# Cosine attention and a low-rank mixer on one core: token tiles regrouped to 3, 1 and twelve pairs, and unit vectors of three batches moved from VectorE to GpSimd

## The chip, the core and the metric

The kernel runs on one core of one Trainium2 chip. The metric is the device time of one execution in microseconds; the median of several runs counts. A profiled execution gives the trace that all tables here come from. "PE" is TensorE's matmul side and "PEld" its weight loads, "DVE" is VectorE, "ACT" ScalarE, "POOL" GpSimd and "SP" the engine that issues most DMAs.

## The reference

Inputs are q, k and v of shape 8 x 12 x 448 x 64 (batch, head, sequence, head dimension), U (448 x 32), V (32 x 448), w1 (768 x 3072) and w2 (3072 x 768), all in fp32.

```
q_n = q / (norm(q) + 1e-6);  k_n = k / (norm(k) + 1e-6)
attn = softmax(q_n @ k_n^T / tau)             # tau = 0.1
x = (attn @ v), heads side by side            # 8 x 448 x 768
u = x + (x^T @ U @ V)^T                       # mixing along the sequence, rank 32
out = u + relu(u @ w1) @ w2
```

## The kernel before

Attention runs batch by batch. For each batch q and k are loaded by GpSimd's DMA queue as tiles of 112 rows (4 sequence positions a row), the squares are made on ScalarE or VectorE, VectorE reduces them, and a square root by logarithm and exponential and a reciprocal give the inverse norms. `norm` (line 690) then multiplies each pair of heads by its inverse norms: two VectorE products of 112 x 512 for each pair (line 702), six pairs a batch. Batches 0 and 1 turn the unit vectors with TensorE transposes (`flip`, line 544); later batches with a DMA transpose issued by SP (line 717). Scores are matmuls with 64 rows (line 763), ScalarE takes the exponential (line 781), values are matmuls with 65 columns whose last column is the sum (line 808), and VectorE divides by it (reciprocal, line 837, and product, line 839).

`stage0` (line 904) makes u from x: a projection with U (line 916), its result A copied to SBUF, matmuls with V (line 967), and an addition to x (line 976). u is stored to DRAM by SP (line 1005) and comes back in two ways: as rows (line 870) and as columns through a DMA transpose (line 866). For batch 1 the columns are made on TensorE instead (`flip` again, its matmuls on line 556), straight into the one buffer `uT`.

Two batches are 896 positions, 7 tiles of 128; the 28 tiles of all batches go through the MLP in units. A *plain* unit (`mlp`, line 1337) has 24 x 6 up matmuls (line 1352) over all its tokens and, for each tile, 2 x 24 down matmuls of 384 columns (line 1394). A *half* unit has two tiles: its up part is plain (144 matmuls of 256 columns, line 1240), and its down part is Strassen-Winograd: 7 products of 12 matmuls of 384 columns (line 1269) in place of 8, with sums of relu blocks (lines 1212 to 1214 and 1223) and of w2 blocks (line 1061). ScalarE copies the first product (line 1292), GpSimd adds u to it three times (line 1294), VectorE adds the other products (line 1287). A *full* unit combines w1 in the same way too (252 up matmuls of 128 columns, line 1133). Before the change the tiles go as two plain units of 3, six half units and five full ones (`PLAIN`, `HALF`). The `relu` buffer and the `uT` buffer are single; `mlp` for one tile puts four blocks of 128 columns into one PSUM bank.

The combined w2 blocks T1, T2, T4 take room that attention no longer needs. The class `Shrink` is a ring of buffers that gives up some of them after a number of uses (`WHOLE` batches); `Gone` is what waits for those uses. T1 lies where two buffers of u rows were, T2 in the third buffer of loaded q and k, in one of unit vectors and in the end of `uT`, T4 in one of squares, two of transposed unit vectors, one of A and a part of `relu`.

The order of all instructions is found ahead of time by a planner (`Plan.run`): each operation has an engine, an assumed duration, dependencies, buffers to acquire and release, and a priority. On PE there are ten streams in order of preference, attention first and the MLP last, so the MLP fills what attention leaves. On GpSimd the additions of line 1294 go ahead of the loads. What the planner gives is one fixed order for each engine, and each engine works through its own in order, waiting where it must. This holds for the issue of DMAs too.

Of the kernel before, what the change touches and what calls it, by code (L numbers as in the profile page):

```python
# [309 lines left out]
def kernel(  # L310
# [27 lines left out]
    PE_BATCHES = 2  # L338
    LATE, VLATE = 6.0, 2.8
    BURST = [1] + [2] + [3] * 6  # L340
    PLAIN = [3, 3]
    HALF = 6
    WHOLE = 4
    LAST = {0: 0, 2: 2, 4: 4}, {0: 0, 2: 0, 4: 4}
    WIDE = 1
    TB = 2
# [18 lines left out]
    def fixed_ring(tiles):  # L365
# [24 lines left out]
    X_t = const.tile([128, 2 * 4 * C], BF, name="X_sb")  # L390
    r_X = fixed_ring([X_t[:, 4 * C * i:4 * C * (i + 1)].rearrange("p (t c) -> p t c", t=4) for i in range(2)])
    A_t = const.tile([128, 3, C], BF, name="A_sb")
    r_A = Shrink([A_t[:, i, :] for i in range(3)], WHOLE, (0, 1))
    r_gone, r_gone2 = Gone(r_ld, r_xn), Gone(r_sq, r_qkT, r_A)
    u_t = const.tile([128, 8, C], BF, name="u_nat")
    r_ur = Shrink([u_t[:, i, :] for i in range(3)], 3, (0, 1))
    dram = ctx.enter_context(tc.tile_pool(name="dram", bufs=1, space=bass.MemoryType.DRAM))
# [4 lines left out]
    w2_t = const.tile([128, NC, C], BF, name="w2_sb")  # L402
    relu_t = const.tile([128, NC * 512], BF, name="relu")
    views = [relu_t.bitcast(FP)[:, 0:4 * R + S + 4 * SC * D]] + [
        relu_t[:, 0:NC * n].rearrange("p (f n) -> p f n", f=NC) for n in (512, 384)] + [None]
    r_relu = Ring(1, lambda i: views[min(i, 3)])
    uv = Slot(r_relu, 6)

# [91 lines left out]
    pe_sc = plan.stream("PE")  # L500
    pe_mlp = plan.stream("PE")
    pool_y = plan.stream("POOL")
    pool_q = plan.stream("POOL")
    plan.keep = pe_sc, r_sc, (0, 1, 2, 3, 4, 5)

# [6 lines left out]
    def dve_t(n, fast=1, fixed=0.065):  # L512
        return fixed + n * 0.00105 / fast
# [176 lines left out]
    def norm(b, p, ld, la, inv, a, deps, pr, loaded):  # L690


        by_pe = b < PE_BATCHES
        first = b == 0 and p == 0
        xn, qkT = Slot(r_xn, 2 if by_pe and (first or (b, p) not in RAW_KEYS) else 1), Slot(r_qkT, SC if b == 0 else sum(p in members(b, x) for x in groups_of(b)))

        def part(i):
            def fn():
                src = ld.tile[:, i, la:la + 2, :].rearrange("p h (c d) -> p h c d", d=D)
                sc = inv.tile[:, i, a:a + 2, :].unsqueeze(3).to_broadcast([SCH, 2, SC, D])  # L700
                dst = xn.tile[:, SC * (1 - i):SC * (2 - i), :].rearrange("p c (h d) -> p h c d", h=2)
                nc.vector.tensor_mul(dst, src, sc)  # L702
            return plan.add(Op("DVE", dve_t(512), fn, deps=[deps[i]], acq=[xn],
                               rel=[getattr(ld, "slot", ld), inv], prio=pr))

        def raw():
            c = Op("ACT/DVE", any_t(512), None, deps=loaded[1], acq=[xn], rel=[ld.slot], prio=-0.9)
            c.fn = lambda: copy_op(
                c, xn.tile[:, 0:SC, :].rearrange("p c (h d) -> p h c d", h=2),
                ld.tile[:, 1, la:la + 2, :].rearrange("p h (c d) -> p h c d", d=D))  # L710
            return plan.add(c)

        keys = (b, p) in RAW_KEYS
        ops = {0: part(0), 1: raw()} if first and keys else {0: part(0)} if keys else {
            i: part(i) for i in ((0, 1) if first else (1, 0))}
        if not by_pe:
            done = [plan.add(Op("SP", 0.1, lambda: nc.sync.dma_start_transpose(
                out=qkT.tile, in_=xn.tile.rearrange("p b e -> p (b e)")), deps=list(ops.values()), acq=[qkT],
                rel=[xn], prio=0, lat=("x", 0.05 * 56, 5.0)))]
        else:  # L720
            done = []
            for i in (1, 0) if keys else ops:
                b0, b1 = SC * (1 - i), SC * (2 - i)
                ins = [(lambda z=z: xn.tile[:, z, :]) for z in range(b0, b1)] if i in ops else [
                    (lambda c=c, hh=hh: ld.tile[:, 1, la + hh, D * c:D * c + D]) for c in range(SC) for hh in range(2)]
                done.append(flip(
                    pe_tp, ins, SCH,
                    lambda: qkT.tile, (lambda t_, x, b0=b0, b1=b1: [(t_[:, b0:b1, :], x)]),
                    [ops[i]] if i in ops else loaded[1], [qkT], [xn if i in ops else ld], len(ins) // SC,
                    "ACT/DVE", 0.05))  # L730
        got[b, p, "qkT"] = (qkT, done, (inv, a, deps[1]))
        return list(ops.values())
# [54 lines left out]
    def values(b, p, X):  # L787
# [39 lines left out]
        for hh in range(2):  # L827
            h = 2 * p + hh
            av, rd = heads[hh][:2]
            o = heads[hh][-1]  # L830
            for t in () if ends else range(4):
                for j in range(SC):
                    first, last = t == 0 and j == 0, t == 3 and j == SC - 1
                    o = plan.add(Op("PE", 0.033 if b < 2 else 0.0305, lambda t=t, j=j, h=h, hh=hh, av=av: product(h, hh, t, j, av, j == 0),
                        deps=exps + got[b, h, "v"] + ready if first else (), acq=([av] if b < 2 else [av, X]) if first else [],
                        rel=([attn, tail] if tail else [attn] if even is attn else [attn, even]) if last else []), pe_av)
            r = plan.add(Op("DVE", 0.20, lambda av=av, rd=rd: nc.vector.reciprocal(
                out=rd.tile, in_=av.tile[:, :, D:D + 1]), deps=[o], acq=[rd], prio=1 if b != 1 else 0.5))
            muls.append(plan.add(Op("DVE", dve_t(256), lambda av=av, rd=rd, h=h: nc.vector.tensor_mul(  # L839
                X.tile[:, :, h * D:(h + 1) * D], av.tile[:, :, 0:D],  # L840
                rd.tile.to_broadcast([128, 4, D])), deps=[r],
                acq=[X], rel=[av, rd], prio=1 if b != 1 else 0.5)))
# [61 lines left out]
    def stage0(b, X, muls):  # L904
# [3 lines left out]
        cols = [(0, 512), (512, 640), (640, C)] if by_pe else [(0, CH), (CH, C)]  # L908
        A = Slot(r_A, 0)
        a_done = []  # L910
        uT = Columns(384 if b == 0 else 512) if by_pe else None
        ut = []
        mms = [Slot(bank, 1) for _ in cols]

# [33 lines left out]
        if b == 0:  # L948
# [2 lines left out]
                s_.uses += 6  # L951
                s_.left += 6
            return us, uT, ut
        for z, (c0, c1) in enumerate(cols):
            for i, t in enumerate(tiles):
                if t < 3:
                    parts = [(A, PAD + 128 * t)]
                elif t == 3:
# [4 lines left out]
                for y, (AA, col) in enumerate(parts):  # L963
                    AA.uses += 1
                    AA.left += 1
                    o = plan.add(Op("PE", pe_t(c1 - c0), lambda y=y, AA=AA, col=col, c0=c0, c1=c1,
                                    mm=mm, last=len(parts) - 1: nc.tensor.matmul(  # L967
                        out=mm.tile[:, 0:c1 - c0], lhsT=V_sb[:, col:col + 128],
                        rhs=AA.tile[:, c0:c1], start=(y == 0), stop=(y == last)),
                        deps=[a_done[z]] if y == 0 else (), acq=[mm] if y == 0 else [], rel=[AA]), pe_a if c1 < C else pe_av)  # L970

                def add(t=t, c0=c0, c1=c1, mm=mm, px=prev.get("X")):
                    w = c1 - c0
# [13 lines left out]
        if by_pe:  # L987
            for ccs in ((0, 1), (2, 3), (4,), (5,)):
                z = max(0, ccs[0] - 3)
                ins = [(lambda i=i, cc=cc: X.tile[:, i, cc * 128:(cc + 1) * 128]) for cc in ccs for i in range(4)]  # L990
                X.uses += 1
                X.left += 1
                ut.append(flip(pe_a if z < 2 else pe_av, ins, 128, lambda: uT.tile,
                               (lambda t_, x, ccs=ccs: [(
                                   t_[:, ccs[0]:ccs[-1] + 1, 0:n],
                                   x.rearrange("p (c i) t -> p c (i t)", c=len(ccs)))]),
                               [adds[z, i] for i in range(len(tiles))], [uT.slot], [X]))
        for i, t in enumerate(tiles):
            x = b // 2, t
            r = slice(64 * par, 64 * par + 64) if t == 3 and b > 1 else slice(0, 128)  # L1000
            X.uses += 1
            X.left += 1
            u_adds[x] = [adds[z, i] for z in range(len(cols))]
            made.setdefault(x, []).append(plan.add(Op(
                "SP", 0.1, lambda x=x, r=r, t=t: nc.sync.dma_start(out=kept[x][r, :], in_=X.tile[r, t - 3 * par, :]),
                deps=u_adds[x], rel=[X], prio=1 if b == 1 else 0, lat=("x", 1.0, 2.0))))
# [37 lines left out]
    def seven_weights(after, tops, downs):  # L1044
# [19 lines left out]
        for j0, j1 in ((0, 3), (3, 6), (6, 8), (8, 10), (10, 12)):  # L1064
            x, n = slice(j0, j1), j1 - j0
            T1, T2, T4 = [home(k, j0, j1) for k in (1, 2, 4)]
            a = minus(T1, B_[:, x, 0, 1], B_[:, x, 0, 0], n, downs[0] + [last_av[2, NPAIR - 1]])
            c = minus(T2, B_[:, x, 1, 1], T1, n, [a, tops[1][-1] if j0 >= 8 else None], [gone])
            d = minus(T4, B_[:, x, 1, 0], T2, n, [c, *(downs[1] if j0 >= 8 else ())], [gone2])
            e = minus(B_[:, x, 0, 1], B_[:, x, 1, 1], B_[:, x, 0, 1], n, [a, *after])  # L1070
            for j in range(j0, j1):
                by[j] = {4: d, 5: a, 6: c, 7: e}
# [489 lines left out]
    n = 0  # L1562
# [66 lines left out]
```

## Time and profile before

| | us |
|---|---|
| median of 3 runs | 555.06 (554.68 to 555.54) |
| the profiled execution | 555.31 |
| its span, first to last instruction | 553.2 |
| PE busy in the span | 544.0 |
| DVE busy | 435.8 |
| ACT busy | 281.5 |
| POOL busy | 141.6 |
| mean granted TensorE clock | 0.996 |

The page of a profile gives these sums, the span in 40 slices of 13.8 us with the busy share of each engine in tenths, the chain of work that ended last with its shares, and rows of instruction groups: line and engine, what is written and read, count, then busy time in total, mean nanoseconds of one, idle time of the engine before them and what ended it. A line such as `L702` is a line of the kernel. The intervals of consecutive matmuls overlap in the rows, so that the price of one in a dense run is read from the chain of waits, where a piece has a start, a length and a count.

### The profile page before, as it was taken

To read this page: it belongs to the slowest core of one execution; us is meant where nothing else is said; L and a number is where in the kernel's file an instruction comes from. 1 tells how busy PE (TensorE), PEld (TensorE's weight loads), DVE (VectorE), ACT (ScalarE), POOL (GpSimd) and SP (SyncE) were. 2 spreads that over 40 slices of the span, in tenths; PEclk is the share of its full clock that TensorE was granted. 3 is DMA by queue.
4 is the path that set the end of the run, shared out by engine and by line. 5 is a ranking of instruction groups with operands and counts; after the bars stand their busy time and mean duration, and the time that the engine had idled before them with its cause. 6 is when DMAs were issued, how large, how long until landed. Compare 5 with 4: busy or idle time off the path is not lost.

```text
span 553.2 us, 14516 instructions
## 1 busy us (share of the span) xinstructions
PE 544.0 (98%) x5974; PEld 383.5 (69%) x5975; DVE 435.8 (79%) x1006; ACT 281.5 (51%) x458; POOL 141.6 (26%) x177
## 2 busy tenths in 40 slices
PE   8899999999999999999999999999999999999996
PEld 6565565655657857767767768668778787878783
DVE  8889968988997688698868979674878585858583
ACT  7876746578637736637746655636214141414140
POOL 8636233143023130531071170110111111111111
PEclk9899999999999999999999999999999999999999
DMA  9999999889459564996298499330231212121201
GB/s 152 202 207 135 205 203 149 148 151 172 81 124 155 64 133 105 106 166 129 58 159 135 113 125 114 95 86 19 63 103 31 87 30 88 31 87 31 87 2 57
DMA packets 140722, 60.66 MB, mean 110 GB/s; under 512 B 99408, under 2 KB 140656, under 8 KB 140656
## 3 DMA queue, kind: packets, MB, share of 16 engines
q0 software_dynamic: 72352, 25.73, 41.5%
q1 hardware_dynamic: 68304, 34.02, 27.8%
q8 instruction: 46, 0.75, 0.6%
q14 instruction: 20, 0.16, 0.1%
HBM read 56.93 MB, written 15.93 MB: 132 GB/s over the span
## 4 chain that ended last, share of the span: by engine, by line
PE 94%; DVE 3%; ACT 1%; DMA 1%; issue 0%; DVEq 0%
PE bank L1269 27%; PE bank L1240 17%; PE bank L1133 13%; PE bank L1352 9%; PE bank L1394 9%; PE bank L808 8%; PE bank L763 7%; PE bank L967 2%; PE bank L556 1%; DVE qk_all L702 1%; ACT attn L776 1%; PE bank L916 1%; DVE ss L634 1%; DMA relu<-in_q_dram 1%; DVE X_sb L839 0%
## 5 line engine op out<-in xcount | busy, mean ns | idle before, releaser
L781 ACT ACTIVATE attn<-bank 128x896 bf16<-128x896 f32 (+1 forms) x163 | 139.7, 915 | 54.2 <-PE bank L763 53.5
L1269 PEld LDWEIGHTS <-relu 128*128 128x128 bf16 x924 | 87.9, 98 | 60.4 <-issue 5.6
L1240 PE MATMUL bank<-uT,w_sb 128*128 128x256 bf16 x864 | 103.2, 273 | 0.0
L1240 PEld LDWEIGHTS <-w_sb 128*128 128x128 bf16 x864 | 81.5, 98 | 17.5 <-issue 7.0
L1269 PE MATMUL bank<-w_sb,relu 128*128 128x384 bf16 x528 | 93.4, 326 | 0.0
L634 DVE TENSOR_REDUCE ss<-sqk 112x8 f32<-112x512 bf16 x96 | 62.0, 671 | 4.7 <-ACT sqk L626 4.4
L702 DVE TENSOR_TENSOR qk_all<-qk_all,inv 112x512 bf16<-112x512 bf16 x93 | 62.8, 703 | 1.6 <-DMA sqk<-qk_all 1.4
L808 PEld LDWEIGHTS <-attn 128*128 128x128 bf16 (+1 forms) x1536 | 54.9, 98 | 7.4 <-issue 3.2
L808 PE MATMUL bank<-v_nat,attn 128*128 128x65 bf16 (+1 forms) x1536 | 57.7, 194 | 0.7 <-DVE X_sb L839 0.3
L578 POOL DMA_DIRECT2D qk_all<-in_q_dram x24 | 17.6, 734 | 157.6 <-issue 68.9
L1394 PE MATMUL bank<-w_sb,relu 128*128 128x384 bf16 x288 | 52.4, 327 | 0.0
L1352 PE MATMUL bank<-uT,w_sb 128*128 128x384 bf16 x288 | 52.1, 327 | 0.0
L763 PE MATMUL bank<-sqk 64*128 64x448 bf16 (+1 forms) x384 | 48.8, 360 | 0.9 <-ACT sqk L1416 0.5
L1250 ACT ACTIVATE relu<-bank 128x512 bf16<-128x512 f32 x51 | 30.5, 597 | 36.9 <-PE bank L1240 36.0
L1133 PEld LDWEIGHTS <-w_sb 128*128 128x128 bf16 x720 | 41.0, 98 | 0.6
L1352 PEld LDWEIGHTS <-w_sb 128*128 128x128 bf16 x288 | 26.6, 98 | 19.1 <-issue 3.4
L1170 ACT COPY attn<-bank 128x512 f32<-128x512 f32 x15 | 8.8, 586 | 60.8 <-PE bank L1133 59.9
L1394 PEld LDWEIGHTS <-relu 128*128 128x128 bf16 x288 | 26.4, 98 | 19.1 <-issue 3.7
L839 DVE TENSOR_TENSOR X_sb<-bank,rd 128x256 bf16<-128x256 f32 x96 | 38.0, 412 | 0.8
L626 ACT ACTIVATE sqk<-qk_all 112x512 bf16<-112x512 bf16 x48 | 29.0, 627 | 16.6 <-DVE ss L634 16.4
L1294 POOL TENSOR_TENSOR relu<-relu,u_nat 128x384 f32<-128x384 f32 x7 | 8.1, 1152 | 110.8 <-ACT relu L1292 110.7
L601 POOL DMA_DIRECT2D v_nat<-in_v_dram x42 | 31.3, 751 | 15.9 <-DMA w_sb<-in_moe_w_ch_dram 12.8
(135 smaller groups left out, 795.1 us busy)
## 6 DMA issues: line engine op xcount, KB each, us to landing
qk_all<-in_q_dram POOLq DMA_DIRECT2D x23, 224.0 KB, 5.5
qk_all<-in_k_dram POOLq DMA_DIRECT2D x23, 224.0 KB, 6.1
u_nat<-u SPq DMA_DIRECT2D x25, 192.0 KB, 3.4
w_sb<-in_moe_w_ch_dram POOLq DMA_DIRECT2D x4, 1152.0 KB, 18.5
w_sb<-in_moe_w_ch_dram POOLq DMA_DIRECT2D x8, 576.0 KB, 15.9
u<-X_sb SPq DMA_DIRECT2D x22, 192.0 KB, 2.0
v_nat<-in_v_dram POOLq DMA_DIRECT2D x11, 168.0 KB, 8.5
out_dram<-O_sb SPq DMA_DIRECT2D x12, 144.0 KB, 2.1
```

The costliest lines, as they stand in the source:

```text
L601: ops = [load(lambda j=j, r0=r0, c=c, s0=s0, s1=s1: nc.gpsimd.dma_start(out=v_t[b % 2][r0:r0 + s1 - s0, :, j, 0:D], in_=src[c, s0:s1]), (s ...
L634: lambda i=i, a0=a0, a1=a1, sq=sq: nc.vector.reduce_sum(ss.tile[:, i, a0:a1, :].rearrange("p h c -> p (h c)"), sq.tile[:, 0:a1 - a0, :].re ...
L702: nc.vector.tensor_mul(dst, src, sc)
L763: nc.tensor.matmul(out=out, lhsT=qkT.tile.rearrange("p b s -> p (b s)")[r, n0:n0 + w], rhs=qkT.tile[r, SC:2 * SC, :].rearrange("p c s -> p ...
L781: exps.append(plan.add(Op("ACT", act_t(2 * S, 0.08), lambda sc=sc, c=c, attn=attn: nc.scalar.activation(out=attn.tile[:, :, off:off + S] i ...
L808: nc.tensor.matmul(out=av.tile[:, t, 0:D + 1], lhsT=tail.tile[:, hh, 128 * t:128 * (t + 1)] if tail and j == SC - 1 else (attn if j < SC - ...
L839: muls.append(plan.add(Op("DVE", dve_t(256), lambda av=av, rd=rd, h=h: nc.vector.tensor_mul(X.tile[:, :, h * D:(h + 1) * D], av.tile[:, :, ...
L1133: o = plan.add(Op("PE", pe_t(128), lambda i=i, j=j, jj=jj: nc.tensor.matmul(out=mm.tile[:, 128 * jj:128 * jj + 128], lhsT=left[k](i, j), r ...
L1240: o = plan.add(Op("PE", pe_t(256), lambda j=j, e=e, cc=cc, mm=mm: nc.tensor.matmul(out=mm.tile[:, 256 * e:256 * e + 256], lhsT=w1_sb[:, cc ...
L1269: o = plan.add(Op("PE", pe_t(CH), lambda j=j: nc.tensor.matmul(out=mm.tile[:, 0:CH], lhsT=left[k](j), rhs=right[k](j), start=(first and j ...
L1352: o = plan.add(Op("PE", pe_t(n), lambda cc=cc: nc.tensor.matmul(out=mm.tile[:, m:m + n], lhsT=w1_sb[:, cc, f * 128:(f + 1) * 128], rhs=uT. ...
L1394: nc.tensor.matmul(out=mm.tile[:, 0:c1 - c0], lhsT=relu.tile[:, f, i * 128:(i + 1) * 128], rhs=w2_t[:, f, c0:c1], start=(f == 0), stop=(f ...
```

## The change

The plain units become one of 3 tiles and one of 1; seven half units follow, then five full ones as before. Of batch 1's u only the tile that the second plain unit takes (tile 3) is transposed on TensorE; the other three come back through DRAM and a DMA transpose. Their additions run over halves of 384 columns, after tile 3's. Twelve products of unit vectors in each of the batches 2, 3 and 4 go to GpSimd in a stream of its own, behind the additions of line 1294 and ahead of the loads. The rings of q and k, unit vectors, squares and transposed unit vectors shrink after three batches instead of four; the ring of A has two buffers from the start. The combined w2 blocks no longer wait for the second plain unit, and for the first values of batch 2 instead of its last. From batch 2 on the planner treats the reciprocal and the product behind the values as one entry.

```diff
-    PLAIN = [3, 3]
-    HALF = 6
-    WHOLE = 4
+    PLAIN = [3, 1]
+    HALF = 7
+    POOL_XN = {2: (0, 1), 3: (0, 1), 4: (0, 1)}
+    WHOLE = 3
...
-    r_A = Shrink([A_t[:, i, :] for i in range(3)], WHOLE, (0, 1))
-    r_gone, r_gone2 = Gone(r_ld, r_xn), Gone(r_sq, r_qkT, r_A)
+    r_A = Shrink([A_t[:, i, :] for i in range(3)], 2, (0, 1))
+    r_gone, r_gone2 = Gone(r_ld, r_xn), Gone(r_sq, r_qkT)
...
+    pool_x = plan.stream("POOL")
     pool_q = plan.stream("POOL")
...
-                nc.vector.tensor_mul(dst, src, sc)
-            return plan.add(Op("DVE", dve_t(512), fn, deps=[deps[i]], acq=[xn],
-                               rel=[getattr(ld, "slot", ld), inv], prio=pr))
+                (nc.gpsimd if pool_ else nc.vector).tensor_mul(dst, src, sc)
+            pool_ = i in POOL_XN.get(b, ())
+            return plan.add(Op("POOL" if pool_ else "DVE", 1.5 if pool_ else dve_t(512), fn, deps=[deps[i]], acq=[xn],
+                               rel=[getattr(ld, "slot", ld), inv], prio=pr), pool_x if pool_ else None)
...
+            if b >= 2:
+                def scale(av=av, rd=rd, h=h):
+                    nc.vector.reciprocal(out=rd.tile, in_=av.tile[:, :, D:D + 1])
+                    nc.vector.tensor_mul(X.tile[:, :, h * D:(h + 1) * D], av.tile[:, :, 0:D],
+                                         rd.tile.to_broadcast([128, 4, D]))
+                muls.append(plan.add(Op("DVE", 0.6, scale, deps=[o], acq=[rd, X], rel=[av, rd], prio=1)))
+                continue
...
-        uT = Columns(384 if b == 0 else 512) if by_pe else None
+        uT = Columns(384 if b == 0 else 128) if by_pe else None
...
-        for z, (c0, c1) in enumerate(cols):
-            for i, t in enumerate(tiles):
+        jobs = [(z, i, t, c0, c1) for z, (c0, c1) in enumerate(cols) for i, t in enumerate(tiles) if b > 1 or t == 3]
+        wide = [(z, i, t, c0, c1) for i, t in enumerate(tiles) for z, (c0, c1) in enumerate(((0, CH), (CH, C))) if b == 1 and t > 3]
+        for jobs in (jobs, wide):
+            for z, i, t, c0, c1 in jobs:
...
-                ins = [(lambda i=i, cc=cc: X.tile[:, i, cc * 128:(cc + 1) * 128]) for cc in ccs for i in range(4)]
+                ins = [(lambda i=i, cc=cc: X.tile[:, i, cc * 128:(cc + 1) * 128]) for cc in ccs for i in range(1)]
...
-            a = minus(T1, B_[:, x, 0, 1], B_[:, x, 0, 0], n, downs[0] + [last_av[2, NPAIR - 1]])
-            c = minus(T2, B_[:, x, 1, 1], T1, n, [a, tops[1][-1] if j0 >= 8 else None], [gone])
-            d = minus(T4, B_[:, x, 1, 0], T2, n, [c, *(downs[1] if j0 >= 8 else ())], [gone2])
+            a = minus(T1, B_[:, x, 0, 1], B_[:, x, 0, 0], n, downs[0] + [last_av[2, 0]])
+            c = minus(T2, B_[:, x, 1, 1], T1, n, [a, tops[0][-1] if j0 >= 8 else None], [gone])
+            d = minus(T4, B_[:, x, 1, 0], T2, n, [c], [gone2])
```

More of the change, by code (lines that the diff above doesn't have):

```diff
@@ L404 @@
     views = [relu_t.bitcast(FP)[:, 0:4 * R + S + 4 * SC * D]] + [
-        relu_t[:, 0:NC * n].rearrange("p (f n) -> p f n", f=NC) for n in (512, 384)] + [None]
+        relu_t[:, 0:NC * n].rearrange("p (f n) -> p f n", f=NC) for n in (384, 128)] + [None]
     r_relu = Ring(1, lambda i: views[min(i, 3)])
@@ L969, in stage0 @@
                         rhs=AA.tile[:, c0:c1], start=(y == 0), stop=(y == last)),
-                        deps=[a_done[z]] if y == 0 else (), acq=[mm] if y == 0 else [], rel=[AA]), pe_a if c1 < C else pe_av)
+                        deps=(a_done if jobs is wide else [a_done[z]]) if y == 0 else (), acq=[mm] if y == 0 else [], rel=[AA]), pe_a if c1 < C or jobs is wide else pe_av)
                 def add(t=t, c0=c0, c1=c1, mm=mm, px=prev.get("X")):
@@ L994, in stage0 @@
                                (lambda t_, x, ccs=ccs: [(
-                                   t_[:, ccs[0]:ccs[-1] + 1, 0:n],
+                                   t_[:, ccs[0]:ccs[-1] + 1, 0:128],
                                    x.rearrange("p (c i) t -> p c (i t)", c=len(ccs)))]),
-                               [adds[z, i] for i in range(len(tiles))], [uT.slot], [X]))
+                               [adds[z, 0]], [uT.slot], [X]))
         for i, t in enumerate(tiles):
@@ L1002, in stage0 @@
             X.left += 1
-            u_adds[x] = [adds[z, i] for z in range(len(cols))]
+            u_adds[x] = [o for (z, k), o in adds.items() if k == i]
             made.setdefault(x, []).append(plan.add(Op(
```

## The prediction

> **What bounds the kernel now.** I read the page first (busy shares, slices, chain), then the windows of engine busy time by stage, then the chain of waits in order of time for the price of one matmul, and last the rows of the operations that the change moves.
>
> ```profile
> PE 544.0 (98%) x5974; PEld 383.5 (69%) x5975; DVE 435.8 (79%) x1006; ACT 281.5 (51%) x458; POOL 141.6 (26%) x177
> ...
> PE   8899999999999999999999999999999999999996
> ...
> DVE  8889968988997688698868979674878585858583
> ACT  7876746578637736637746655636214141414140
> POOL 8636233143023130531071170110111111111111
> ...
> PE 94%; DVE 3%; ACT 1%; DMA 1%; issue 0%; DVEq 0%
> ```
>
> TensorE is busy in 98% of the span and makes 94% of the chain that ended last. The other 6% (33 us) is the start, before about 40 us, and a short tail. VectorE comes second, at 8 to 9 tenths until slice 26 (about 370 us), while attention still runs.
>
> ```profile
> 70.00:106.24 36.24, 36.08 (x370) 22.33 (x370) 30.22 (x74) 18.02 (x30) 9.78 (x14) 1.00 1.14 169
> 106.24:170.80 64.56, 64.56 (x605) 37.24 (x604) 56.49 (x127) 41.22 (x70) 19.57 (x28) 1.00 0.96 136
> 170.80:210.20 39.40, 39.40 (x437) 28.12 (x436) 32.00 (x75) 23.64 (x38) 7.19 (x9) 1.00 0.75 116
> ```
>
> These are three stretches of the windows view (length, then PE, PEld, DVE, ACT and POOL busy, granted clock). PE fills each to 0.2 us or better. So the time is the sum of TensorE's work, and an edit counts only if it changes that sum or opens a gap in it.
>
> ```profile
> 100.73 0.78 PE bank L556 x12
> 106.24 1.62 PE bank L1352 x10
> 160.92 3.68 PE bank L1394 x22
> 173.48 2.73 PE bank L1240 x25
> 410.20 14.07 PE bank L1133 x252
> 535.15 13.66 PE bank L1269 x84
> ```
>
> The chain (start, length, count) prices one step on PE: 0.1625 us per 384-column matmul (1.62/10, 13.66/84), 0.1085 per 256-column one (173.48 row; 2.73/25 is 0.109), 0.0558 per 128-column one (14.07/252), 0.055 to 0.065 per transpose (0.78/12 is the high end). The group rows' means (273, 326 ns) overlap and are not used.
>
> **What the skill says.** "TensorE: Matmul & The Clock Gate", § "Wait — 56ns, not 53.3ns?", gives N/2.4 GHz plus about 2.5 ns per warm matmul: 55.8, 109.2 and 162.5 ns, which this trace confirms, so a 128-column matmul is no worse than pro rata here, weight load included. "GPSIMD Engine Reference", § "3.1 Elementwise — side-by-side cycle accounting", states 2.6 cycles per element for two inputs; an estimate for 512 elements at its 1.2 GHz is 1.1 us plus dispatch. "SBUF — State Buffer", § "SBUF: two separate sides", says that a GpSimd operation and a VectorE one with two SBUF inputs exclude each other for a whole instruction. The rows below fit both.
>
> ```profile
> L702 DVE TENSOR_TENSOR qk_all<-qk_all,inv 112x512 bf16<-112x512 bf16 x93 | 62.8, 703 | 1.6 <-DMA sqk<-qk_all 1.4
> L628 POOL TENSOR_TENSOR sqk<-qk_all 112x512 bf16<-112x512 bf16 x4 | 4.1, 1039 | 1.9 <-DVE ss L634 1.7
> L1294 POOL TENSOR_TENSOR O_sb<-relu,u_nat x17: 904/910/2569, 197.4 to 485.7; 128x384 f32<-128x384 f32 x17
> L866 SPq DMA_TRANSPOSE uT<-u x22: 1211/1234/2249, 137.3 to 505.5; - x22
> 111.50 19.40 SPq L717 DMA_TRANSPOSE sqk<-qk_all  x6
> 127.11 1.25 POOL L606 DMA_DIRECT2D v_nat<-in_v_dram  x2 [2.00 <-DMA v_nat<-in_v_dram]
> ```
>
> The first two are group rows, the next two come from the views of one line (minimum/median/maximum ns), the last two from the timelines of SP and GpSimd.
>
> **Part 1, units 3+1 and seven half units.** A plain unit of 3 tiles does 144 up and 144 down matmuls of 384 columns: 288 x 0.1625 = 46.8 us. A half unit (plain up, combined w2) does 144 x 0.1085 + 84 x 0.1625 = 15.6 + 13.65 = 29.3. The new one-tile unit does 144 x 0.0558 + 48 x 0.1625 = 8.0 + 7.8 = 15.8. Taken out: one 3-tile unit, 46.8. Put in: 15.8 + 29.3 = 45.1. **Minus 1.7 us.** The five full units stay.
>
> **Part 2, batch 1's u.** 24 transposes on PE become 6: 18 x 0.056 to 0.065 = **minus 1.0 to 1.1 us**, all on the path. The low-rank matmuls of tiles 4 to 6 become 2 of 384 columns each instead of 512 + 128 + 128: 0.325 against 0.327 us a tile, nothing. Their adds and the PSUM copies (two of 1.0 us on ScalarE, about 1 us more) shrink by some 2 us beside PE: nothing. SP gets two more uT transposes (24 for 22, 1.23 us each of its queue).
>
> **Part 3, unit vectors by GpSimd.** 36 multiplications (12 in each of three batches) leave VectorE: 36 x 0.703 = 25.3 us off it. GpSimd's row for a product of a broadcast scale doesn't exist. Lower bound: the squares of the same shape, 1.04; upper: the longest of L1294, 2.57. I take 1.2 (0.910 x 512/384). 36 x 1.2 = 43 us, about 14 us in a batch's 45 to 50, where GpSimd is 2 to 3 tenths busy. It costs nothing on PE while SP's transposes, which wait for these products, still issue in time. Queued behind them on GpSimd are q, k and v loads; ahead of them, load issues that stall on earlier DMAs (2.0 us at 127.11).
>
> **Part 4, VectorE in sum.** The extra half unit brings 12 sums of 0.35, 2 of 0.555, 6 bank adds of 0.555 and some 3.5 relu of 0.687: 11.0 us. The smaller second unit drops about 4.3 us of relu and 4 adds of 0.55. Net plus 4.5, minus 25.3, minus about 1: **VectorE is about 22 us lighter**. It isn't the bound, so I count no gain, only cover. Reciprocal and multiply of batches 2 to 7 planned as one entry are the same instructions: nothing.
>
> **Part 5, earlier weights, shallower rings.** The combined w2 (L1061, 20 operations, about 12 us of VectorE, 148 to 176 us now) is wanted a plain-unit remainder earlier. The second unit now ends near 105 + 15.8/0.74 = 127 us (0.74 is PE's share for the MLP: 23.4 of the 31.5 us from 106.24 to 137.7); the first half unit's down starts near 148, its product with T4 near 160. The ring edits free T2's and T4's room after batch 2 instead of 3: batch 2's last values ran at 146, its scores before 138. About 20 us of cover, and the reliefs of part 4: nothing. Without it PE would wait on product 6, 7 or 4. Batch 3 with two buffers in place of three works as batches 4 to 7 do already. The A ring of two makes batch 2 wait for batch 0's last reader, in the first unit's up, long past. Each later tile is wanted when it was before, as the MLP has done the same tiles by then.
>
> **Sum.** 1.7 + 1.0 = 2.7 us less PE work. The profiled execution took 555.31 us (553.2 of span and 2.1 around it), 0.25 over the median of 555.06. 555.31 - 2.7 = 552.6; against the median **552.4 us**.
>
> **Rivals.** *Starved first half unit (slower).* Now the first tile that comes back through a DMA transpose is wanted at 170.9 and was there at about 163. In the new order tiles 4 and 5 of batch 1 are wanted near 127; their transposes can start when the second unit's up frees the one uT buffer, near 105 + 8.0/0.74 = 116, and land at 122 (two of 1.23 us, 3.2 to landing). Cover: 5 us. But SP is in order, and from 111.5 to 131 it carried six L717 transposes, 3.2 us apart, that wait for the very products that go to GpSimd. At 1.2 us a pair takes 2.4 us, within 3.2. At 2.57 a pair takes 5.1, six are 11.5 us late, and less 5 of cover PE stops for 6.5: about 559. It decides from a lateness of 5 + 2.7 + 1.1, some 9 us. For it: the 2.57 us instances, VectorE's density here, load stalls ahead in GpSimd's queue. Against: the median of L1294 is 0.91. *Small gaps eat it (same).* One product waits 2 to 3 us for T4 or for a batch's u: 554.4 to 555.4. For: VectorE is at 88% from 106 to 171 us (56.5 of 64.6) and the weights come last in its order. Against: its relief falls on that stretch. *The change doesn't do what it says*: the order comes from a planner, which may put the freed VectorE time to attention alone. PE's sum falls all the same, so this ends like the first forecast. A gain beyond 2.7 would have to come from the start's 4.4 us of PE idle, which nothing here touches: bound 551.4.
>
> **How the numbers follow.** No gaps, 552.4 (own range 551.6 to 553.4): 0.70. Small gaps, about 555: 0.13, of which 0.04 stays faster, 0.08 is the same and 0.01 slower. Starved, 556.5 to 562: 0.17, all slower. What this kernel's measurement can tell from no change is 0.2%, 1.1 us. Faster 0.74, same 0.08, slower 0.18. The range 551.4 to 557.2 leaves out the far end of the starved case and a little below.
>
> **What would show it.** Right: windows with PE full from 40 to about 407 us; the first L1133 block near 407.5; 1008 matmuls on L1240; 6 transposes of X_sb on L556; 36 L702 products on GpSimd near 1.2 us; 57 on VectorE; combined weights on L1061 between 110 and 150. Wrong: PE idle charged to DMA uT or to L1061's tiles between 115 and 170; GpSimd products above 2 us; SP waiting long on L717 ahead of uT.

## The result and the profile after

| | median us | runs | ratio to before, 95% interval |
|---|---|---|---|
| before, beside the first comparison | 555.14 | 20 | |
| changed kernel, first comparison | 553.18 (551.35 to 556.22) | 20 | 0.9975 (0.996 to 0.999) |
| the same kernel again | 555.37 (551.81 to 557.31) | 16 | 1.0009 (0.9997 to 1.0022) |
| the same kernel, a third time | 555.90 (552.40 to 557.79) | 14 | 1.0009 (0.9993 to 1.0026) |

The ratios are of means. Beside the two later comparisons the kernel before had medians of 554.87 (29 runs) and 554.70 (19 runs).

The first comparison falls where the forecast put it: 553.18 against 552.4, faster by 0.25%. The two later ones show no change. All 50 runs of the changed kernel have a median of 554.7 and spread over 6.4 us; the 68 of the kernel before beside them spread over 2.6. Eleven of the 50 lie under 553: nine of the 20 of the first comparison, one of 16 and one of 14 of the others. What decides this share, no run shows. The question is therefore two questions: did the 2.7 us arrive, and what takes them back in most runs. The profiled execution took 556.2 us (span 554.4), at the upper end, so it shows the second.

From the page of the changed kernel, sums, slices and chain:

```profile
PE 543.1 (98%) x6086; PEld 390.9 (71%) x6086; DVE 432.2 (78%) x979; ACT 279.9 (50%) x457; POOL 182.4 (33%) x216
...
PE   8899998999999999999999999999999999999996
...
PE 93%; DVE 4%; ACT 1%; DMA 1%; issue 0%; DVEq 0%
```

TensorE still fills 98%, but its seventh slice (83 to 97 us) now reads 8, and VectorE has a point more of the chain. The windows by stage (length, then PE, PEld, DVE, ACT, POOL busy, granted clock) say how much:

```profile
70.00:110.53 40.53, 38.04 (x361) 22.57 (x359) 30.26 (x67) 17.77 (x34) 23.35 (x28) 0.96 1.09 159
110.53:170.00 59.47, 59.47 (x687) 42.58 (x684) 49.53 (x108) 36.92 (x59) 28.93 (x31) 1.00 0.89 130
170.00:212.00 42.00, 42.00 (x481) 29.75 (x478) 33.44 (x79) 23.87 (x40) 26.26 (x31) 1.00 1.05 128
```

Between 70 and 110 us PE stands idle for 2.5 us and its clock averages 0.96, where it had 1.00 before; everything after is full. The chain of waits in that place (start, length, count):

```profile
89.35 0.56 DVE O_sb L1417
89.91 3.68 DVE sqk L632
93.58 1.19 DVE ss L636 x2
94.77 0.16 DVE rd L847 x2
94.93 0.40 DVE X_sb L849
...
95.38 1.92 PE bank L811 x32
```

One VectorE square of 112 x 512 takes 3.68 us where the others take 0.42. Behind it in VectorE's queue are two reductions and then the division of a value block, and TensorE's next value block waits for that. That block then takes 1.92 us; such a block takes 0.97 to 1.00 everywhere else in this chain. The windows of one microsecond each show why: the granted clock (third number from the end) falls to a half.

```profile
95.00:96.00 1.00, 0.62 (x12) 0.62 (x12) 0.97 (x4) 0.79 (x3) 0.00 (x0) 0.71 0.74 143
96.00:97.00 1.00, 1.00 (x23) 1.00 (x21) 1.00 (x4) 0.29 (x1) 0.73 (x1) 0.50 0.08 16
97.00:98.00 1.00, 1.00 (x12) 0.51 (x10) 0.66 (x2) 0.60 (x2) 1.00 (x2) 0.50 0.00 0
98.00:99.00 1.00, 1.00 (x5) 0.41 (x4) 0.48 (x1) 0.00 (x0) 1.00 (x2) 0.59 0.00 0
```

It is 1.00 on both sides of these four. What is missing in them adds up to 1.7 us of clock (0.29 + 0.50 + 0.50 + 0.41), which is 3.4 us at half speed. The timeline of the stop shows what ran beside the square:

```profile
89.25 4.04 POOL L704 TENSOR_TENSOR qk_all<-qk_all,inv 112x512 bf16<-112x512 bf16 x4
89.35 0.56 DVE L1417 TENSOR_TENSOR O_sb<-bank,u_nat 128x384 f32<-128x384 f32 x1 [0.35 <-PE bank L1406]
...
89.82 3.76 DVE L632 TENSOR_TENSOR sqk<-qk_all 112x512 bf16<-112x512 bf16 x1
...
95.38 1.92 PE L811 MATMUL bank<-v_nat,attn 128*128 128x65 bf16 x32 [2.49 <-DVE X_sb L849]
```

Four of the moved products run back to back on GpSimd from 89.25 to 93.29. The square, which reads its tile from SBUF as both of its inputs, ends 0.3 us after the last of them. The addition on line 1417, one input of which is in PSUM, passes in its usual 0.56 us while GpSimd multiplies. That is what the Trainium skill states in "SBUF — State Buffer", § "SBUF: two separate sides": GpSimd and a VectorE operation with two SBUF inputs exclude each other. What it adds here is the length: the square got no turn between the four products.

### The profile page after: what moved, and what is told of

It reads as the page before. It is cut to its first block, busy times and chain, and to the rows that moved or that the text cites. A ratio compares the mean times of both kernels' runs of the same rounds, so it can differ in the third digit from the quotient of the medians.

```text
span 554.4 us, 14781 instructions
## 1 busy us (share of the span) xinstructions
PE 543.1 (98%) x6086; PEld 390.9 (71%) x6086; DVE 432.2 (78%) x979; ACT 279.9 (50%) x457; POOL 182.4 (33%) x216
## 4 chain that ended last, share of the span: by engine, by line
PE 93%; DVE 4%; ACT 1%; DMA 1%; issue 0%; DVEq 0%
PE bank L1281 30%; PE bank L1252 20%; PE bank L1145 13%; PE bank L811 8%; PE bank L766 7%; PE bank L1364 6%; PE bank L1406 5%; PE bank L979 2%; DVE qk_all L704 1%; DVE ss L636 1%; ACT attn L779 1%; PE bank L926 1%; PE bank L558 1%; DVE sqk L632 1%; DMA relu<-in_q_dram 1%; DVE X_sb L849 0%
## 5 line engine op out<-in xcount | busy, mean ns | idle before, releaser
L1281 PEld LDWEIGHTS <-relu 128*128 128x128 bf16 x1008 | 95.8, 98 | 65.5 <-issue 6.0
L1252 PE MATMUL bank<-uT,w_sb 128*128 128x256 bf16 x1008 | 120.6, 273 | 0.0
L1252 PEld LDWEIGHTS <-w_sb 128*128 128x128 bf16 x1008 | 95.1, 98 | 20.8 <-issue 8.7
L1281 PE MATMUL bank<-w_sb,relu 128*128 128x384 bf16 x576 | 102.4, 326 | 0.0
L704 POOL TENSOR_TENSOR qk_all<-qk_all,inv 112x512 bf16<-112x512 bf16 x36 | 39.7, 1130 | 36.0 <-DVE inv L658 35.9
L1145 PEld LDWEIGHTS <-w_sb 128*128 128x128 bf16 x720 | 41.0, 98 | 0.6
L628 ACT ACTIVATE sqk<-qk_all 112x512 bf16<-112x512 bf16 x52 | 31.4, 632 | 19.1 <-DVE ss L636 19.1
L704 DVE TENSOR_TENSOR qk_all<-qk_all,inv 112x512 bf16<-112x512 bf16 x57 | 39.0, 721 | 0.3
L1364 PE MATMUL bank<-uT,w_sb 128*128 128x384 bf16 (+1 forms) x288 | 35.6, 273 | 0.0
L1406 PE MATMUL bank<-w_sb,relu 128*128 128x384 bf16 x192 | 35.3, 328 | 0.0
L1299 DVE TENSOR_TENSOR O_sb<-bank,O_sb 128x384 f32<-128x384 f32 x35 | 19.3, 556 | 17.8 <-PE bank L1281 10.5
L843 DVE TENSOR_TENSOR X_sb<-bank,rd 128x256 bf16<-128x256 f32 x72 | 30.6, 425 | 2.5
```

Of the source, the lines that this page charges most:

```text
L704: (nc.gpsimd if pool_ else nc.vector).tensor_mul(dst, src, sc)
L1145: o = plan.add(Op("PE", pe_t(128), lambda i=i, j=j, jj=jj: nc.tensor.matmul(out=mm.tile[:, 128 * jj:128 * jj + 128], lhsT=left[k](i, j), r ...
L1252: o = plan.add(Op("PE", pe_t(256), lambda j=j, e=e, cc=cc, mm=mm: nc.tensor.matmul(out=mm.tile[:, 256 * e:256 * e + 256], lhsT=w1_sb[:, cc ...
L1281: o = plan.add(Op("PE", pe_t(CH), lambda j=j: nc.tensor.matmul(out=mm.tile[:, 0:CH], lhsT=left[k](j), rhs=right[k](j), start=(first and j ...
L1364: o = plan.add(Op("PE", pe_t(n), lambda cc=cc: nc.tensor.matmul(out=mm.tile[:, m:m + n], lhsT=w1_sb[:, cc, f * 128:(f + 1) * 128], rhs=uT. ...
L1406: nc.tensor.matmul(out=mm.tile[:, 0:c1 - c0], lhsT=relu.tile[:, f, i * 128:(i + 1) * 128], rhs=w2_t[:, f, c0:c1], start=(f == 0), stop=(f ...
```

## The experiments

**The changed kernel again** (`again`), no edit.

> The changed kernel once more, to see how its times spread and whether its profile varies. Theory A (the sum of TensorE's work fell by 2.7 us; in some executions four GpSimd products in a row shut out a VectorE square for 3 to 4 us near 90 us, and TensorE then stops for 2.5 us and runs slower for 1.5): times between 551.4 and 556.2, the median at 552 to 554; a profile with a time near 552 shows no square above 2 us at that place, one near 556 shows it again. Theory B (the spread comes from DMA landing times at the start or around the batch 2 loads): same times, but the profile shows the square at 0.4 us and the difference at another place.

Median 555.37, above the 552 to 554 that was expected; ratio 1.0009. Its profile (a run of 554.99, span 553.2) has the long square too, and a longer collision at 142 us, where a sum of relu blocks (line 1226) meets four more products. From the timelines of the two places:

```profile
88.36 4.04 POOL L704 TENSOR_TENSOR qk_all<-qk_all,inv 112x512 bf16<-112x512 bf16 x4
88.69 4.00 DVE L632 TENSOR_TENSOR sqk<-qk_all 112x512 bf16<-112x512 bf16 x1
...
142.11 4.20 POOL L704 TENSOR_TENSOR qk_all<-qk_all,inv 112x512 bf16<-112x512 bf16 x4
142.12 2.29 DVE L1226 TENSOR_TENSOR relu<-relu 128x384 bf16<-128x384 bf16 x1
...
146.12 1.19 PE L811 MATMUL bank<-v_nat,attn 128*128 128x65 bf16 x32 [0.83 <-DVE X_sb L843]
```

PE lost 2.73 us at the first place and 0.83 at the second, but its clock stayed at 1.00 afterwards. In the first profile the same sum took 1.27 us and PE did not stop there. So two things vary between executions: how long the second collision lasts, and whether the clock falls after the stop. In the Trainium skill, "TensorE: Matmul & The Clock Gate", § "Part 1: The HAM clock gate (the "warmup" mystery)", says that at least one idle window of about 3.4 us halves the clock, that a busy one restores it, and that these windows run free of the kernel. The half (0.50) and the 3.4 us at it agree with that. The condition does not: the stop of the first profile was 2.49 us, shorter than such a window. What decides whether the clock falls, no run here shows.

The mean clock of each execution is on record for all 50 runs. In 18 of them it is 0.994 or less, and these take 555.6 to 557.8 us; in the other 32 it is higher, and they take 551.4 to 556.2. In 91 runs of the kernel before it is never below 0.995. So the fall of the clock belongs to the upper end of the spread. No run of the changed kernel near 552 was profiled: that these are the runs without the stop is argued from `swap2` below, not shown.

**Batch 2's unit vectors back on VectorE** (`pool34`).

```diff
-    POOL_XN = {2: (0, 1), 3: (0, 1), 4: (0, 1)}
+    POOL_XN = {3: (0, 1), 4: (0, 1)}
```

> The changed kernel with the unit vectors of batch 2 back on VectorE; batches 3 and 4 stay on GpSimd. Theory A: no stop near 90 us, 551.6 to 552.8 in every run, ratio 0.994 to 0.996, narrow. Theory B: the spread of 551.4 to 556 stays, ratio 0.9975. A third outcome, VectorE too full in batch 2 without the relief: other gaps of TensorE between 100 and 170 us, above 553.

556.32 us, ratio 1.0029 (1.0017 to 1.0040): the third outcome. The stop near 90 us is gone, as theory A says, but a half unit waits 2.2 us for a uT transpose at 168 us (the chain leads back through the stores to VectorE's additions to x on line 988) and 0.8 for a relu on VectorE at 192.

**No unit vectors on GpSimd** (`nopool`): `POOL_XN = {}`.

> The changed kernel with all unit vectors on VectorE, so only the regrouping and what belongs to it. If the gain is TensorE's sum alone, and the relief of VectorE is mere cover: 552.0 to 553.0, ratio 0.995 to 0.997, narrow. If VectorE's 25 us are needed to keep the order free of gaps: 554 or more, with TensorE idle charged to VectorE between 110 and 210 us.

556.68 us, ratio 1.0029 (1.0019 to 1.0039). The windows show the gaps in another place:

```profile
140.00:170.00 30.00, 27.66 (x275) 17.71 (x274) 26.42 (x60) 17.17 (x30) 7.38 (x10) 0.99 0.99 137
170.00:212.00 42.00, 41.57 (x463) 29.26 (x461) 34.38 (x81) 20.61 (x33) 12.40 (x17) 0.97 0.84 119
```

PE is idle for 2.8 us and runs at 0.97 for 42 us (1.3 us), with VectorE at 88% from 140 to 170. The regrouping alone does not pay: without the relief its order has gaps worth more than its gain. The timeline names three short waits of the scores for an exponential at 166 to 169 us, and in the chain that leads up to them are additions to x, bank additions and reductions on VectorE:

```profile
167.92 0.36 PE L766 MATMUL bank<-sqk 64*128 64x448 bf16 x2 [1.27 <-ACT attn L784]
```

**Squares of batch 2 planned on ScalarE** (`actsq2`, and once more as `actsq2b`).

The end of the line that calls `scales`:

```diff
-... "ACT/DVE" if b != 1 else "DVE", hold, then)
+... "ACT" if b == 2 else "ACT/DVE" if b != 1 else "DVE", hold, then)
```

> The changed kernel with the squares of batch 2 on ScalarE only, so that in batch 2 VectorE has hardly an instruction with two SBUF inputs while GpSimd multiplies. Theory A: the long instruction is gone, 551.6 to 553.0, ratio 0.994 to 0.996. Theory B: spread and ratio as in the changed kernel. If ScalarE becomes the late one: TensorE idle on exponentials, above 554.

> The changed kernel planned with the squares of batch 2 on ScalarE, once more: its first five runs had a median of 552.27. If that holds it is the best version: 551.9 to 553, ratio 0.994 to 0.997. If it was luck of those runs: 553.5 to 555.

552.27 and 551.98 us, ratios 0.9955 (0.9943 to 0.9967) and 0.9947 (0.9934 to 0.9959); all ten runs lie between 551.45 and 553.56. This beats both kernels, and most of the spread is gone. As the planner makes another order with it, it does not yet prove the cause. Its trace has a collision too, a square of 2.85 us at 106 us beside two products, and PE stays full from 104 to 112: this collision cost nothing, as TensorE did not yet need what was queued behind it.

**The kernel before with the 36 products on GpSimd** (`beforepool`): the lines of `norm` and `pool_x` of the change put into the kernel before, nothing else.

> The kernel before with only the 36 products moved to GpSimd; tiles stay 3 and 3. Theory A (the move is cover for VectorE and a source of collisions, the gain is the regrouping's): TensorE's sum is unchanged, so 554.5 to 555.5 without a collision, up to 559 with the stop near 90 us; ratio 1.000 to 1.006. Rival C (the relief of VectorE itself is worth time): below 553.5.

559.28 us, ratio 1.0085 (1.0058 to 1.0111), a little above the upper end. In the order that the planner makes with it, the move costs time. Its timeline has the same collision:

```profile
88.66 4.73 DVE L632 TENSOR_TENSOR sqk<-qk_all 112x512 bf16<-112x512 bf16 x1
89.05 4.05 POOL L704 TENSOR_TENSOR qk_all<-qk_all,inv 112x512 bf16<-112x512 bf16 x4
...
95.18 1.13 PE L811 MATMUL bank<-v_nat,attn 128*128 128x65 bf16 x32 [3.47 <-DVE X_sb L842]
```

Here the square is recorded 0.4 us ahead of the first product and still ends behind the last. Spans on GpSimd are rough, so who came first is not settled by this.

**The kernel before with batch 2's squares on ScalarE** (`beforeact`), the edit of `actsq2`.

> The kernel before with the squares of batch 2 on ScalarE only: a control for the run that did the same to the changed kernel. Theory A: nothing to avoid here, as no GpSimd product runs then; 554.5 to 555.5, ratio 0.999 to 1.001. Rival D (ScalarE squares are better by themselves): about 552.5.

556.44 us, ratio 1.0038 (1.0020 to 1.0055). That speaks against rival D: in this kernel the edit is no gain. Theory A's number was missed as well, since the new order has a wait of 1.5 us for uT and smaller ones.

**Only the q products of batch 2 on GpSimd** (`half2`): `POOL_XN = {2: (0,), 3: (0, 1), 4: (0, 1)}`.

> The changed kernel with only the q products of batch 2 on GpSimd, its k products on VectorE; batches 3 and 4 as they are. Theory A: no four products in a row near 90 us, so no VectorE instruction shut out for over 2.5 us there; TensorE not stopped there by more than 1 us. If six products of relief suffice: 552 to 553.5. If batch 2 needs all twelve: gaps from 120 to 200 us as with none, 555 to 556.

554.33 us, ratio 0.9987 (0.9980 to 0.9994), all 16 runs within 2 us, between the two ranges expected. No long stop near 90; in its place waits of 0.7 us at 99 and 0.6 at 110, both behind VectorE. Narrow, but only partly better.

**Squares of batches 2 to 4 on ScalarE** (`actsq234`).

> The changed kernel with the squares of batches 2, 3 and 4 on ScalarE only. Theory A: as with batch 2 alone, 551.7 to 553, perhaps 0.3 us better if batches 3 and 4 have small collisions left. If ScalarE's exponentials become late: TensorE idle charged to ScalarE, 554 or more.

556.06 us over 22 runs (553.69 to 559.26), ratio 1.0016: a miss. The one profiled execution was its fastest run, with waits of 1.0 us for a relu and 0.9, in two parts, for divisions, all VectorE's. The wait for the relu has a collision ahead of it, though no square is left on VectorE in these batches:

```profile
135.68 4.04 POOL L704 TENSOR_TENSOR qk_all<-qk_all,inv 112x512 bf16<-112x512 bf16 x4
136.54 3.41 DVE L1224 TENSOR_TENSOR relu<-relu 128x384 bf16<-128x384 bf16 x1 [0.78 <-ACT relu L1262]
...
141.27 1.14 PE L1252 MATMUL bank<-uT,w_sb 128*128 128x256 bf16 x9 [1.02 <-DVE relu L1264]
```

A sum of relu blocks, 0.35 us elsewhere, ends 0.2 us after the last of four products, and the relu stands behind it. What its other runs lose is open.

**The changed kernel's own order, four squares on ScalarE** (`swap2`), beside the changed kernel (`again2`) on the same chip. The edit is in what is issued, not in what is planned; the instructions of TensorE, GpSimd and SP and their order are unchanged, VectorE's list is short of four squares and ScalarE's has them.

```diff
-                    if o.by == "ACT":
+                    if o.by == "ACT" or b == 2:
```

> The changed kernel in its own order, with the four VectorE squares of batch 2 executed by ScalarE at their places; nothing else moves (the instruction lists of TensorE, GpSimd and SP are the same). Theory A (a square with two SBUF inputs is shut out by four GpSimd products in a row): TensorE's stop near 90 us is gone, 551.5 to 553, ratio 0.994 to 0.997; what is left is a stop near 142 us of under 1 us. Rival E (the order itself is short of VectorE time there, whichever engine squares): TensorE still waits over 2 us near 92 us, about 555.

> The changed kernel beside the run that differs from it by four squares alone, on the same chip. Theory A: 553 to 555.5, wider than the other, with the long square in the profile. If its times here lie at 552.5, the stop depends on more than the order, and the comparison settles little.

552.04 us (551.65 to 553.28), ratio 0.9955 (0.9941 to 0.9968), against 555.90 for the unedited kernel, which is 0.4 above the range expected for it. Four squares, 2.3 us of ScalarE's 282, are worth 3.9 us by the medians and 3.1 by the means. The stop expected to remain near 142 us is absent: the sum there takes 1.29 us. From the timeline of `swap2`:

```profile
88.78 4.05 POOL L704 TENSOR_TENSOR qk_all<-qk_all,inv 112x512 bf16<-112x512 bf16 x4
89.41 2.19 ACT L628 ACTIVATE sqk<-qk_all 112x512 bf16<-112x512 bf16 x4
...
92.14 1.14 PE L811 MATMUL bank<-v_nat,attn 128*128 128x65 bf16 x32
```

and of `again2`:

```profile
88.94 4.04 POOL L704 TENSOR_TENSOR qk_all<-qk_all,inv 112x512 bf16<-112x512 bf16 x4
89.15 4.13 DVE L632 TENSOR_TENSOR sqk<-qk_all 112x512 bf16<-112x512 bf16 x1
...
95.07 1.57 PE L811 MATMUL bank<-v_nat,attn 128*128 128x65 bf16 x32 [2.86 <-DVE X_sb L849]
```

GpSimd runs its four products in both, for the same 4.05 us. With the square elsewhere the reductions and the division behind it run while GpSimd multiplies, and the value block starts 3 us earlier. Rival E is out, and theory A is shown for the stop: the square shut out by the products is its cause.

**Units of 3 and 3, products on GpSimd, the same swap** (`bpswap`): the edit of `swap2` on `beforepool`.

> Units of 3 and 3 with the 36 products on GpSimd, in that kernel's own order, its four VectorE squares of batch 2 executed by ScalarE. Theory A: the 3.5 us stop near 90 us and the slow stretch after it go, 4 to 5 us less than the 559.28 measured with the VectorE squares: 554.5 to 556. The regrouped kernel with the same swap should lie 2.7 us lower, if TensorE's sum is the rest of the difference. Rival E: above 558.

557.31 us, ratio 1.0056: 2.0 less than 559.28, where 4 to 5 was expected. The two medians come from different comparisons of six runs each; counted from the first dense block of the first unit's up, the profiles differ by 3.3 (518.16 and 514.86 us). The stop of 3.47 is gone; a new wait of 0.57 for A stands beside it, and the order's other waits (0.43, 0.55 and 0.25 us at 133, 183 and 286) remain. The expected slow stretch of clock was not in `beforepool`'s profile in the first place (1.13 us for the block). So the two groupings with the swap differ by 5.3 us, not by 2.7. The four waits named add up to 1.8; the remainder is not accounted for.

## Why the prediction was right, and where it was not

**The sum of TensorE's work: right.** The 2.7 us are read best from `swap2`, where no single stop of PE after the start reaches 0.25 us. The start varies by about 1 us between executions, so count from the first dense block of the first unit's up. From the chain of waits of `swap2`:

```profile
40.34 7.64 PE bank L1364 x47
...
407.37 14.07 PE bank L1145 x252
```

Its span is 550.2, so 509.86 us from that block on; before, the block stood at 40.66 of 553.2, 512.54. The difference is 2.68, against 1.7 + 1.0 forecast (the upper end given for part 2 should read 1.2, as 18 x 0.065); PE's busy time in these two stretches differs by 2.50 (507.77 and 505.27). The one-tile unit's matmuls ran at 0.0557 us (this line is from the changed kernel's chain):

```profile
110.53 2.34 PE bank L1364 x42
```

**The stop: its size was foreseen, its place and cause were not.** The rival of small gaps had a wait of 2 to 3 us, for T4 or a batch's u. Part 3 said that the moved products cost nothing on PE "while SP's transposes, which wait for these products, still issue in time". That step failed. I had quoted the exclusion between the two engines, used it only for how long a product might take, and asked only who waits for the product. The cost fell on VectorE's side: an instruction of 0.42 us took 3.8 to 4.1, and what was queued behind it in order was the division that TensorE needed. In the profiled run it cost 2.5 us of idle PE and 1.7 us of clock, 4.2 together. Counted from its first dense block, at 40.91, that run is 513.49 us long, 3.6 more than `swap2`, which itself keeps 0.4 us of small gaps between 89 and 95 us. `again`, with its block at 39.78, is 513.42 long, 3.6 more as well, with stops of 2.73 and 0.83. By this account a run reads about 552 without the stop and 555 to 556 with it.

**The product's price: close.** 1.2 us was taken, with 2.57 as the upper bound:

```profile
L704 POOL TENSOR_TENSOR qk_all<-qk_all,inv 112x512 bf16<-112x512 bf16 x36 | 39.7, 1130 | 36.0 <-DVE inv L658 35.9
L704 DVE TENSOR_TENSOR qk_all<-qk_all,inv 112x512 bf16<-112x512 bf16 x57 | 39.0, 721 | 0.3
```

1.13 on the mean (median 1.04), 36 moved and 57 left, as counted. One product took 3.50, above the bound and a sign that the prediction had named as one of being wrong. It began at 132.34 and ended at 135.84, beside a square and four of the combined w2 that VectorE ran one behind the other, and PE did not stop:

```profile
131.34 6.85 POOL L704 TENSOR_TENSOR qk_all<-qk_all,inv 112x512 bf16<-112x512 bf16 x4 [22.05 <-DVE inv L658]
...
132.58 2.35 DVE L1073 TENSOR_TENSOR w_sb<-w_sb 128x1152 bf16<-128x1152 bf16 x4
```

**VectorE's relief: mis-sized.** The row of VectorE that was read as 8 to 9 tenths has sixes and sevens in it too. Forecast was 22 us lighter. In `swap2` it is 435.8 - 428.1 = 7.7, and that run has four squares fewer. By group rows, added over their shapes: the products did leave (63.5 to 39.7 us), but the sums of relu blocks rose from 42.9 to 50.9 where 4.2 was allowed, and the planner gave VectorE ten more relu of half units (14.4 to 21.4 us) instead of 3.5 more. Of the sums, some 4 us are longer instructions, as `nopool` has the same 43 of each at 46.8. As the relief was cover and not gain, the time did not move with it. That it was needed as cover, `nopool` and `pool34` make likely: with fewer products on GpSimd they lose over 4 us against `swap2`. Their orders differ in more than that, so this is not shown alone.

**The starved half unit: did not happen.** The transposes for the first half unit went out in time; SP's timeline of the changed kernel:

```profile
121.24 2.54 SPq L876 DMA_TRANSPOSE uT<-u  x2
```

The second lands by 126, and the unit starts at 131.7: the 5 us of cover forecast, never used up. The combined w2 was made from 117 to 136 us, within the forecast's 110 to 150, and no product waited for it. The range held because its upper end covered a stop of this size, though for another reason. That the first comparison came out within 0.8 us of 552.4 was in part luck, as nine of its 20 runs lie under 553 and only two of the 30 later ones; the later medians are 3.0 and 3.5 us above the forecast. The chance of 0.08 for "no change" was too small for a kernel whose runs fall on both sides of it.

## What to carry to other kernels

When work moves from VectorE to GpSimd, list the VectorE instructions with two SBUF inputs that will stand beside it, and what is queued behind each of them: the price is paid there, and can be as long as the whole burst on GpSimd, not one instruction. Put the colliding instruction on ScalarE, if it is one that ScalarE can do; here four squares decided 3 to 4 us. Whether breaking up the burst does as well was not settled: `half2` did that and gained less. When a kernel's runs begin to spread after a change, one profile shows one branch: take several, and swap the suspected instruction inside the same order before trusting a version that replans everything.

## What was not expected of the hardware

The wait of a VectorE instruction was as long as the burst: four products of 1.0 us back to back held the square for 3.3 to 4.3 us beyond its 0.42, in four profiles of two kernels, and a sum in `actsq234` for 3.1 us. In the other collision, near 142 us, a sum got its turn after one product (1.27 and 1.29 us in the first profile and `swap2`) or two (2.29 in `again` and `again2`). The first profile shows it the other way round too: beside a square and four instructions of the combined w2 on VectorE, one product took 3.50 us in place of 1.04. And stops of TensorE of 2.7 and 3.5 us (`again`, `beforepool`) cost nothing more, while stops of 2.5 and 2.9 us (the first profile, `again2`) each cost 1.7 us of clock on top.
